# Pairs of heads normalised in one go, row maxima turned by VectorE, ten buffers of exponentials and an order written out as ranks, in a fused attention, soft-MoE and MLP kernel

## The chip, the core and the metric

One core of a Trainium2 chip runs one launch of the program. The metric is the device time of a run in microseconds; the profile gives the span from the first to the last instruction of one profiled execution. PE is TensorE's matmul side, PEld its weight loads, DVE VectorE, ACT ScalarE, POOL GpSimd, SP SyncE, whose queue issues most of the DMAs in its own order.

## The reference

```python
# q, k, v: [4, 8, 576, 64]
q_rot, k_rot = (rotate(q), rotate(k))                  # rotary embedding, halves of 32
scores = np.matmul(q_rot, k_rot.transpose(0, 1, 3, 2)) / np.sqrt(64)
attn = np.exp(scores - np.max(scores, axis=-1, keepdims=True))
attn = attn / (np.sum(attn, axis=-1, keepdims=True) + 1e-09)
x = np.matmul(attn, v)                                 # then [2304, 512], heads side by side
logits = x @ phi                                       # 32 slots: 8 experts x 4
d = softmax(logits, over tokens)                       # with 1e-09 in both sums
slot_out[e] = np.maximum((d.T @ x)[e] @ w1[e], 0.0) @ w2[e]   # e = 0..7, F = 1024
x = softmax(logits, over slots) @ slot_out
h = np.maximum(x @ w_in, 0.0)                          # w_in 512 x 2048, 64-bit words in memory
out = (h * h) @ w_out
```

## The kernel before

Attention works on sixteen pairs of heads (a batch has four). The two heads of a pair lie on partitions 0 to 63 and 64 to 127. The 576 keys are four blocks of 128 and a tail of 64, the 576 queries two halves of 288. One pair is nine units in the order of `SEQ`: blocks 0 to 3 for the first half, the tail for both halves (`BOTH`), blocks 0 to 3 for the second half. Rotary products are made on POOL (L424), rounded to a high part by ACT (L458), and the rest is kept as a low part.

For each unit three things run on PE. `max_unit` (L535) makes approximate scores from the high parts alone, and DVE reduces them to column maxima (L546). `st_unit` makes the scores from high and low parts (L607) and subtracts the row's maximum by one more matmul against `pick` (L614); ACT takes the exponential (L627) into one of the buffers `prs`. `pv_unit` multiplies an exponential with v (L655, the tail L650) into one of two PSUM banks, one for each half.

Between them stand smaller steps. `max_rows`, once a pair (twice in the first), reduces the maxima over the blocks (L558), turns the 128×10 result on PE (L565), copies it out on DVE with the second operand of the tail (L571, L576; `keep_apart` is a constant for that), and two DMAs put the row into `mrow` (L584), which the scores of this pair read. `norm`, once a half, lets PE sum the exponentials over the keys against ones (L676, eight calls), after POOL has added units 0 and 1 into an accumulator in `pb` (L635). DVE then transposes the sums in PSUM (L682), adds 1e-9 (L688), adds four quadrants crosswise (four L690), takes the reciprocal (L691), spreads it back by a transpose (L702) and multiplies (L698) into `xT`. `logits` then multiplies `xT` with phi (L726, L731) and turns it on PE (L749); `slots_in`, once a batch, forms the softmax over tokens and the slots' inputs (L794, L832). The experts (L1375, L1437) and the MLP (L1612, L1682) follow; their weights are loaded by SP into the buffers that attention gives up (L1002).

The order on every engine is made when the program is built. `Plan` holds all steps with the engine, the estimated length, what they read and write, and a due time, and emits at each moment the most urgent one that can start. `retime` sets the due times from tables (`TABLE`, `SHIFT`) and `STAY` lets PE prefer steps of the kind that it is in: r for approximate and exact scores, c and b for products with v, q for sums and logits, f for turning. Three pieces of PSUM, the ring, are taken by every step of PE that DVE or ACT reads afterwards, and given back by the reader. Buffers: six of exponentials for the blocks and two for the tail, and two accumulators in `pb`; `p_slot` numbers them round.

## Time and profile before

| | |
|---|---|
| runs, us | 569.60, 569.64, 570.91 (median 569.64) |
| span of the profiled execution, us | 567.9 |
| mean granted TensorE clock | 0.999 |
| busy, us: PE, PEld, DVE, ACT, POOL | 550.7, 419.7, 387.5, 285.4, 220.2 |
| DMA | 85.69 MB, mean 151 GB/s |

The profile is of one execution. The order in which to read it: the 40 slices and the windows by stage say which engine is full in which stretch; PE's timeline in one stretch gives the price of a step as the distance from one start to the next (ends of matmuls are modelled and overlap); the chain of waits says what the last instruction was waiting for, backwards; the groups give the mean time of one operation. Attention takes about the first 290 us, the experts the next 50, the MLP the rest.

### The profile page before, as it was taken

The numbers are of one execution on the slowest core, as the hardware profiler recorded it, in microseconds if no ns is written. First come the engines' busy times: TensorE is split into PE (matmuls) and PEld (weight loads), VectorE is DVE, ScalarE is ACT, GpSimd is POOL, SyncE is SP. The second block draws the span as 40 slices with busy tenths as digits, with TensorE's granted clock in tenths as the row PEclk, the third lists the DMA queues.
The fourth block names the chain that finished last, engine by engine and source line by source line (L and its number), as shares of the span: only waits on it lengthen the run. The fifth ranks groups of instructions, "written<-read, shape, count | busy, mean of one in ns | idle before, by whom it ended". The sixth has DMA issues, their size and how long they took to land.

```text
span 567.9 us, 13319 instructions
## 1 busy us (share of the span) xinstructions
PE 550.7 (97%) x5466; PEld 419.7 (74%) x5466; DVE 387.5 (68%) x845; ACT 285.4 (50%) x533; POOL 220.2 (39%) x173
## 2 busy tenths in 40 slices
PE   4999999999999999999999999999999999999996
PEld 3656666576666667666743348999999999999996
DVE  6587788888888877867475137975785595554553
ACT  2334455664565664534423247975944564454440
POOL 4999999987888888621200000000000000000000
PEclk9999999999999999999999999999999999999999
DMA  6547796867784356254669997142200220000333
GB/s 235 145 127 195 167 241 183 227 176 202 200 232 109 103 145 178 99 174 172 211 249 387 386 395 258 47 146 76 75 1 1 74 75 1 1 2 1 113 113 112
DMA packets 41838, 85.69 MB, mean 151 GB/s; under 512 B 12176, under 2 KB 12848, under 8 KB 40624
## 3 DMA queue, kind: packets, MB, share of 16 engines
q1 hardware_dynamic: 41494, 84.24, 47.9%
q8 instruction: 43, 0.70, 0.5%
q10 hardware_dynamic: 282, 0.59, 0.4%
q14 instruction: 19, 0.16, 0.1%
HBM read 77.92 MB, written 6.82 MB: 149 GB/s over the span
## 4 chain that ended last, share of the span: by engine, by line
PE 84%; DMA 5%; DVE 5%; POOL 2%; ACT 1%; issue 1%; SPq 0%; DVEq 0%
PE bank L1682 35%; PE bank L607 11%; PE obank L655 11%; PE bank L535 5%; PE bank L676 5%; PE bank L614 3%; PE obank L1612 3%; PE bank L1375 3%; DVE mcol L546 2%; DMA tEb<-in_w_dram 2%; DMA tLb<-in_w_in_dram 2%; PE obank L650 2%; PE bank L749 2%; DMA ident<-in_ident_dram 1%; POOL arena L424 1%; PE bank L726 1%
## 5 line engine op out<-in xcount | busy, mean ns | idle before, releaser
L627 ACT ACTIVATE tO<-bank 128x576 f32<-128x576 f32 x144 | 86.4, 650 | 87.0 <-PE bank L614 82.5
L546 DVE TENSOR_REDUCE mcol<-bank 128x2 f32<-128x576 f32 x144 | 103.2, 747 | 20.0 <-PE bank L535 10.0
L424 POOL TENSOR_TENSOR arena<-arena 128x576 f32<-128x576 f32 x78 | 110.9, 1441 | 8.1 <-DMA arena<-in_qk_dram 6.7
L1682 PE MATMUL bank<-w,tEb 128*128 128x256 f32 x864 | 106.6, 279 | 0.1
L1682 PEld LDWEIGHTS bank<-w,tEb 128*128 128x128 f32 x864 | 103.7, 188 | 2.3 <-issue 1.6
L655 PE MATMUL obank<-tO,pb 128*64 128x288 f32 x512 | 76.2, 419 | 0.0
L635 POOL TENSOR_TENSOR pb<-tO 128x576 f32<-128x576 f32 x32 | 45.7, 1429 | 36.2 <-ACT tO L627 34.4
L1682 PE MATMUL bank<-w,tEa 128*128 128x256 f32 x432 | 53.0, 278 | 0.0
L1682 PEld LDWEIGHTS bank<-w,tEa 128*128 128x128 f32 x432 | 51.6, 188 | 1.2 <-issue 1.2
L1682 PE MATMUL bank<-w,tO 128*128 128x256 f32 x432 | 51.6, 277 | 0.0
L1682 PEld LDWEIGHTS bank<-w,tO 128*128 128x128 f32 x432 | 51.1, 188 | 0.0
L655 PEld LDWEIGHTS obank<-tO,pb 128*64 128x64 f32 x512 | 31.1, 136 | 23.7 <-issue 9.5
L1623 ACT ACTIVATE pb<-obank 128x384 f32<-128x384 f32 x47 | 21.7, 494 | 38.0 <-PE obank L1612 37.9
L1623 ACT ACTIVATE w__1093<-obank 128x384 f32<-128x384 f32 x48 | 21.8, 492 | 36.9 <-PE obank L1612 36.6
L676 PE MATMUL bank<-tO,ones 128*32 128x288 f32 x256 | 36.7, 409 | 0.0
L535 PEld LDWEIGHTS bank<-tEb 64*128 64x128 f32 x180 | 16.3, 184 | 21.2 <-DVE mcol L546 4.2
L535 PE MATMUL bank<-tEb 64*128 64x288 f32 x180 | 30.8, 355 | 0.7 <-DVE mcol L546 0.5
L424 POOL TENSOR_TENSOR tLb<-arena,tEb 128x576 fp32r<-128x576 f32 x20 | 28.7, 1450 | 1.3 <-ACT tEb L458 1.3
L607 PE MATMUL bank<-tEb 64*128 64x288 f32 x180 | 28.3, 310 | 0.3 <-DVE mcol L546 0.2
L1612 PE MATMUL obank<-x,tO 128*128 128x384 f32 x95 | 26.8, 337 | 0.5 <-DVE tO L1540 0.5
L682 DVE STREAM_TRANSPOSE bank<-bank 128x288 f32<-128x288 f32 x32 | 15.9, 496 | 15.9 <-PE bank L676 15.8
L607 PE MATMUL bank<-tLb,tEb 64*128 64x288 f32 x180 | 26.6, 292 | 0.0
(309 smaller groups left out, 1066.8 us busy)
## 6 DMA issues: line engine op xcount, KB each, us to landing
arena<-in_qk_dram SPq DMA_DIRECT2D x14, 576.0 KB
arena<-in_qk_dram SPq DMA_DIRECT2D x12, 512.0 KB
arena<-in_w_dram SPq DMA_DIRECT2D x8, 512.0 KB
pb<-in_v_dram SPq DMA_DIRECT2D x12, 320.0 KB
arena<-in_qk_dram SPq DMA_DIRECT2D x3, 1152.0 KB
tLb<-in_w_in_dram SPq DMA_DIRECT2D x3, 1024.0 KB
pb<-in_w_in_dram SPq DMA_DIRECT2D x3, 1024.0 KB
w__450<-in_w_dram SPq DMA_DIRECT2D x4, 512.0 KB
```

The costliest lines, as they stand in the source:

```text
L424: ENG[e].tensor_tensor(out=o, in0=x, in1=y, op=how)
L535: nc.tensor.matmul(on_ring(tok)[:, j, 0:HQ], lhsT=x[rows], rhs=hi[rows, 0, HALF[c]], start=(u < BOTH or c == 0), stop=(u < BOTH or c == 1),)
L546: lambda e: nc.vector.tensor_reduce(out=mcol[:, h, :, u], in_=on_ring(tok)[:, :, 0:HQ], op=ALU.max, axis=AX.X),
L607: nc.tensor.matmul(st[:, j, 0:HQ], lhsT=w[rows], rhs=q[y][rows, HALF[c]], start=(i == 0 and (u < BOTH or c == 0)), stop=False,)
L614: nc.tensor.matmul(st[:, j, 0:HQ], lhsT=pick[rows, w : w + 128], rhs=mrow[rows, HALF[c]], start=False, stop=(u < BOTH or c == 1),)
L627: lambda e: nc.scalar.activation(out=pr, in_=on_ring(tok)[:, :, 0:HQ], func=AF.Exp, scale=0.125),
L635: lambda e: nc.gpsimd.tensor_tensor(out=acc, in0=one, in1=pr, op=ALU.add),
L655: nc.tensor.matmul(BANKS[6 + h][o, 0:HQ], lhsT=vr[:, u, j, :], rhs=pr[:, j, :], start=(h == 0 and u == 0), stop=(h == 1 and u == 3))
L676: nc.tensor.matmul(sm[QUAD[2 * j + w], 0:HQ], lhsT=one, rhs=xs_[2 * i + w][:, j, :], start=(i == 0), stop=(i == 1))
L1612: lambda e, i=i, t0=t0: nc.tensor.matmul(BANKS[i][:, 0:384], lhsT=wst_of()[:, 128 * fc : 128 * fc + 128], rhs=cst_of()[:, t0 : t0 + 384], ...
L1623: lambda e, i=i, h=h: nc.scalar.activation(out=rg_of()[:, 0, h], in_=BANKS[i][:, 0:384], func=AF.Relu),
L1682: nc.tensor.matmul(BANKS[c][:, cols], lhsT=gt[:, x, 128 * c : 128 * c + 128], rhs=wo[:, fc % 2, y, cols], start=(fc % FQ == 0 and i == 0 a ...
```

## The change

- **Order.** `retime` no longer moves due times by tables; it replaces each by a tenth of a rank out of `ORDER`, a list for each kind of step, engine and PE kind. `STAY` is gone.
- **Maxima.** `max_rows` stays on DVE: the tail's second operand is folded in by one more reduction, the result is turned by four 32×32 transposes, and the DMAs read that tile. The transpose on PE, the two copies, and `keep_apart` with its two instructions go.
- **Buffers.** `prs` has ten buffers: eight in the two `tO` tiles and two in `pb`, where the accumulators were. `slot_of` deals them out from a list; a buffer is given back early where POOL has added its contents into another. A score unit's matmuls now wait for the buffer's readers too.
- **Additions.** `fold` replaces the accumulators: POOL adds unit n into the buffer of unit 0, in place, for n below `folded(p)`: 2 for pairs 0 to 11, 4 for 12 to 14, 3 for the last. 46 additions stand for 32.
- **Norm.** Once a pair, after its last unit: one run of sums (16 matmul calls, 8 in pairs 12 to 14, 12 in the last), one transpose, the columns read out of PSUM by one instruction for both halves and four of 32 partitions, one reciprocal; then for each half the transpose back and the multiplication.

```diff
-    STAY = 20.522
+    ORDER = {
...
+        ("max_rows", "DVE", None): (
+            45, 55, 121, 216, 251, 336, 485, 597, 612, 688, 810, 895, 988, 1119, 1185, 1285, 1303
+        ),
...
-            kind, last = self.kinds[i] or (None, False)
-            key = (kind, "/".join(sorted(o[0])), {"b": "c"}.get(o[10], o[10]))
-            due = o[2]
-            if key in self.UNITS:
-                table, more, ahead = self.UNITS[key]
-                n = count[key] = count.get(key, -1 - ahead) + 1
-                if due >= -8 and (table != "mx" or n >= -3):
-                    due = n + self.TABLE[table + " last" if last and table != "mx" else table][n % 9] + more
-            elif due >= -8:
-                due += self.SHIFT.get((*key, last), self.SHIFT.get((*key, False), 0.0))
-            self.ops[i] = (*o[:2], due, *o[3:])
+            kind = self.kinds[i] and self.kinds[i][0]
+            key = (kind, "/".join(sorted(o[0])), kind and o[10])
+            n = count[key] = count.get(key, -1) + 1
+            ranks = self.ORDER.get(key, {})
+            if kind or n in ranks:
+                self.ops[i] = (*o[:2], 0.1 * ranks[n], *o[3:])
...
-                return o[2] - (self.STAY if c[3] == "PE" and o[10] is not None and o[10] == mode else 0.0), c[1], c[2]
+                return self.ops[c[2]][2], c[1], c[2]
...
-    NHI, NLO, NPR, NRING = 3, 3, 6, 10
+    NHI, NLO, NPR, NRING = 3, 3, 10, 10
...
-    accs = [view(pb, S * i, [128, 2, HQ]) for i in range(2)]
-    prs = [view(tos[i // 4], S * (i % 4), [128, 2, HQ]) for i in range(8)]
+    prs = [view(tos[i // 4], S * (i % 4), [128, 2, HQ]) for i in range(8)] + [view(pb, S * i, [128, 2, HQ]) for i in range(2)]
...
-            [ck], take="ring", tok=tok, mode="r",
+            [ck, (mk, u, h)], take="ring", tok=tok, mode="r",
...
     def max_rows(p, g, us=slice(0, 5)):
-        mr, mrk = small("mrow", [10, 128], F32R, bufs=2)
-        m10, m10k = small("m10", [128, 10])
+        mt, mtk = small("mrow", [32, 128], bufs=2)
         mcol, mk = mcols[p]
-        tok = {}
-        marks["r0"] = op(
-            {"DVE": 0.15},
-            lambda e: nc.vector.tensor_reduce(
-                out=m10.rearrange("p (j u) -> p j u", j=2)[:, :, us], in_=mcol.rearrange("p h j u -> p j u h")[:, :, us], op=ALU.max, axis=AX.X
-            ),
-            g + T["mrdve"], [(mk, u, h) for u in range(5)[us] for h in range(2 if u < BOTH else 1)], [m10k],
-        )
-        op(
-            {"PE": 0.11},
-            lambda e: nc.tensor.transpose(on_ring(tok)[0:10, 0, 0:128], m10, ident),
-            g, [m10k, "ident"], [("rw", p)], take="ring", tok=tok, mode="f",
-        )
-        op(
-            {"DVE": 0.25},
-            lambda e: nc.vector.tensor_scalar(out=mr, in0=on_ring(tok)[0:10, 0, 0:128], scalar1=1.0, scalar2=None, op0=ALU.mult),
-            g + T["mrdve"], [("rw", p)], [mrk],
-        )
-        marks["r1"] = ring_op(
-            {"DVE": 0.2},
-            lambda e: nc.vector.scalar_tensor_tensor(
-                out=mr[:, 0:64], in0=on_ring(tok)[0:10, 0, 64:128], scalar=keep_apart, in1=f(mr)[:, 0:64], op0=ALU.add, op1=ALU.max
-            ),
-            g + T["mrdve"], ["apart", ("rw", p)], [mrk], give="ring", tok=tok,
+        last = us.stop == 5
+        def turned(e):
+            if last:
+                nc.vector.tensor_reduce(out=mcol[0:64, 1, :, BOTH], in_=mcol[64:128, 0, :, BOTH].unsqueeze(2), op=ALU.max, axis=AX.X)
+            nc.vector.tensor_reduce(
+                out=m10[:, 0:10].rearrange("p (j u) -> p j u", j=2)[:, :, us], in_=mcol.rearrange("p h j u -> p j u h")[:, :, us], op=ALU.max, axis=AX.X
+            )
+            for a in range(4):
+                nc.vector.transpose(out=mt[:, 32 * a : 32 * a + 32], in_=f(m10)[32 * a : 32 * a + 32])
+        marks["r0"] = marks["r1"] = op(
+            {"DVE": 1.14 if last else 0.97}, turned,
+            g + T["mrdve"], [(mk, u, h) for u in range(5)[us] for h in range(2 if u < BOTH else 1)], ["m10", mtk],
         )
...
+    slot_of, idle, given = [], list(range(NPR)), []
+    def folded(p):
+        return 2 if p < NP - 4 else 4 if p < NP - 1 else 3
+    for n in range(NP * len(SEQ)):
+        p, i = divmod(n, len(SEQ))
+        idle += [x for t, x in given if t <= n]
+        given = [(t, x) for t, x in given if t > n]
+        slot_of.append(idle.pop(0))
+        u = SEQ[i][1]
+        given.append((n + 4 if 0 < u < folded(p) else 9 * p + 12, slot_of[-1]))
+        given.sort()
     def p_slot(p, h, u):
-        i = (8 * p + 4 * h + u) % NPR if u < BOTH else NPR + p % 2
+        i = slot_of[len(SEQ) * p + SEQ.index((h if u < BOTH else None, u))]
         return prs[i], ("P", i)
...
-            [ck], take="ring", tok=tok, mode="r",
+            [ck, pk], take="ring", tok=tok, mode="r",
...
-        if u == 1:
-            acc, ak = accs[(2 * p + h) % 2], ("acc", (2 * p + h) % 2)
-            one, k1 = p_slot(p, h, 0)
-            op(
-                {"POOL": 1.39},
-                lambda e: nc.gpsimd.tensor_tensor(out=acc, in0=one, in1=pr, op=ALU.add),
-                g + 0.6, [k1, pk], [ak],
-            )
...
+    def fold(p, h, n, s):
+        (pr, pk), (other, k) = p_slot(p, h, 0), p_slot(p, h, n)
+        op(
+            {"POOL": 1.39}, lambda e: nc.gpsimd.tensor_tensor(out=pr, in0=pr, in1=other, op=ALU.add),
+            s + n + 0.6, [k], [pk],
+        )
+    def norm(p, g):
+        things = [p_slot(p, None, BOTH)] + [[p_slot(p, h, u) for h in range(2)] for u in (0, *range(folded(p), 4))]
         tok = {}
         QUAD = [slice(32 * i, 32 * i + 32) for i in range(4)]
         def sums(e):
             sm = on_ring(tok)[:, 0]
-            xs_ = [acc] + [x for x, _ in rest]
-            for i in range(2):
+            for i, x in enumerate(things):
                 for j in range(2):
-                    for w in range(2):
-                        one = half_ones[:, h] if i and w else ones[:, 0:32]
+                    for h in range(2):
+                        one, pr = (ones[:, 0:32], x[h][0]) if i else (half_ones[:, h], x[0])
                         nc.tensor.matmul(
-                            sm[QUAD[2 * j + w], 0:HQ], lhsT=one, rhs=xs_[2 * i + w][:, j, :], start=(i == 0), stop=(i == 1)
+                            sm[QUAD[2 * j + h], 0:HQ], lhsT=one, rhs=pr[:, j, :], start=(i == 0), stop=(i == len(things) - 1)
                         )
-        op({"PE": 0.97}, sums, g + T["sums"], [("acc", n)] + [k for _, k in rest], [("sm", n)], take="ring", tok=tok, mode="q")
+        keys = [things[0][1]] + [k for x in things[1:] for _, k in x]
+        op({"PE": 0.485 * len(things)}, sums, g + T["sums"], keys, [("sm", p % 2)], take="ring", tok=tok, mode="q")
         op(
-            {"DVE": 0.47}, lambda e: nc.vector.transpose(out=on_ring(tok)[:, 1, 0:HQ], in_=on_ring(tok)[:, 0, 0:HQ]),
-            g, [], [("sm", n)],
-        )
-        def inverse(e):
-            col = on_ring(tok)[:, 1, 0:HQ].rearrange("p (b c) -> p b c", c=32)[:, :, 0:1]
-            nc.vector.tensor_scalar(out=r9, in0=col, scalar1=1e-9, scalar2=None, op0=ALU.add)
+            {"DVE": 0.5}, lambda e: nc.vector.transpose(out=on_ring(tok)[:, 1, 0:HQ], in_=on_ring(tok)[:, 0, 0:HQ]),
+            g, [], [("sm", p % 2)],
+        )
+        def columns(e):
+            col = on_ring(tok)[:, 1, 0:HQ].rearrange("p (b c) -> p c b", c=32)[:, 0:1]
+            nc.vector.tensor_scalar(out=r18, in0=col.to_broadcast([128, 2, HQ // 32]), scalar1=1e-9, scalar2=None, op0=ALU.add)
             for q in range(4):
-                nc.vector.tensor_tensor(out=r9[QUAD[q]], in0=r9[QUAD[q]], in1=col[QUAD[q ^ 1]], op=ALU.add)
-            nc.vector.reciprocal(out=r9, in_=r9)
-        def scaled(e):
+                nc.vector.tensor_scalar(out=r18[QUAD[q], 1 - q % 2], in0=col[QUAD[q ^ 1], 0], scalar1=1e-9, scalar2=None, op0=ALU.add)
+        def scaled(e, h):
             parts = [(slice(0, 128), 0, HQ, HQ * h)]
             if p < TURNED:
                 parts = [(HEADS[0], 0, HQ, HQ * h)] + [(HEADS[1], a, b, (HQ * h + a - 64) % S) for a, b in (((0, 64), (64, HQ)) if h == 0 else ((0, HQ),))]
             for rows, a, b, to in parts:
                 nc.vector.tensor_tensor(out=xT[rows, to : to + b - a], in0=BANKS[6 + h][rows, a:b], in1=recT[rows, a:b], op=ALU.mult)
-        ring_op({"DVE": 1.1}, inverse, g, [("sm", n)], ["r9"], give="ring", tok=tok)
-        op(
-            {"DVE": 0.48}, lambda e: nc.vector.transpose(out=recT, in_=r9.to_broadcast([128, HQ // 32, 32])),
-            g, ["r9"], ["recT"],
-        )
-        op(
-            {"DVE": 0.8 if p < TURNED else 0.4},
-            scaled,
-            g, [("O", h), "recT"], [("xT", h)],
-        )
+        ring_op({"DVE": 0.8}, columns, g, [("sm", p % 2)], ["r18"], give="ring", tok=tok)
+        op({"DVE": 0.27}, lambda e: nc.vector.reciprocal(out=recs, in_=r18), g, ["r18"], ["r9"])
+        for h in range(2):
+            op(
+                {"DVE": 0.48}, lambda e, h=h: nc.vector.transpose(out=recT, in_=recs[:, h].unsqueeze(2).to_broadcast([128, HQ // 32, 32])),
+                g + 0.1 * h, ["r9"], ["recT"],
+            )
+            op(
+                {"DVE": 0.8 if p < TURNED else 0.4},
+                lambda e, h=h: scaled(e, h),
+                g + 0.1 * h, [("O", h), "recT"], [("xT", h)],
+            )
...
-            if n in ENDS:
-                at(s + LAG + 0.1, norm, p, ENDS[n], s + T["norm"])
+            if u == 0:
+                for i in range(1, folded(p)):
+                    at(s + LAG + 0.5, fold, p, h, i, s)
+        at(g0 + NU - 1 + LAG + 0.1, norm, p, g0 + NU - 1 + T["norm"])
...
```

How the order moves, at three places. In its rows `tEa`, `tEb` and `tLa`, `tLb` are the high and the low parts of the rope results, `es` stands in the matmuls that only fill PE's time, `obank` is a bank of products with v, `tO` and `pb` hold exponentials, `w__` a load buffer. A count behind a row stands for like rows.

PE at the start, before, from the first pair's tail maxima on:

```order
L535 MATMUL bank_93<-tEa,wins 128x288 x2
L565 MATMUL bank_91<-ident,m_115 10x128
L1756 MATMUL obank_94<-es 128x128 x4
L565 MATMUL bank_91<-ident,m_115 10x128
L607 MATMUL bank_92<-tEa 128x288 x2
L607 MATMUL bank_92<-tLa,tEa 128x288 x2
L607 MATMUL bank_92<-tEa,tLa 128x288 x2
L614 MATMUL bank_92<-tEb,pick 128x288 x2
L607 MATMUL bank_93<-tEa 128x288 x2
L607 MATMUL bank_93<-tLa,tEa 128x288 x2
L607 MATMUL bank_93<-tEa,tLa 128x288 x2
L614 MATMUL bank_93<-tEb,pick 128x288 x2
```

and after the change:

```order
L644 MATMUL bank_93<-tEa,wins 128x288 x2
L1863 MATMUL obank_94<-es 128x128 x6
L719 MATMUL bank_91<-tEa 128x288 x2
L719 MATMUL bank_91<-tLa,tEa 128x288 x2
L719 MATMUL bank_91<-tEa,tLa 128x288 x2
L726 MATMUL bank_91<-tEb,pick 128x288 x2
L719 MATMUL bank_93<-tEa 128x288 x2
L719 MATMUL bank_93<-tLa,tEa 128x288 x2
L719 MATMUL bank_93<-tEa,tLa 128x288 x2
L726 MATMUL bank_93<-tEb,pick 128x288 x2
L644 MATMUL bank_92<-tEb 128x288 x2
L644 MATMUL bank_91<-tEb 128x288 x2
```

The two transposes of the maxima (L565) are gone from PE, and behind the second score unit (`bank_93`) stand maxima of the next pair (L644 on `tEb`), where before the third of five score units followed.

POOL at the start, before, from the second low part of pair 1 (`tLb`) on; L635 is the addition of exponentials:

```order
L424 TENSOR_TENSOR tLb<-arena,tEb 128x576
L424 TENSOR_TENSOR arena<-arena,w__134 128x576
L635 TENSOR_TENSOR pb<-tO_83 128x576
L424 TENSOR_TENSOR arena<-arena 128x576
L424 TENSOR_TENSOR arena<-arena,w__134 128x576
L424 TENSOR_TENSOR tLb<-arena,tEb 128x576
L424 TENSOR_TENSOR arena<-arena,w__134 128x576
L635 TENSOR_TENSOR pb<-tO_84 128x576
L424 TENSOR_TENSOR arena<-arena 128x576
L424 TENSOR_TENSOR arena<-arena,w__134 128x576
L424 TENSOR_TENSOR tLb<-arena,tEb 128x576
```

and after, with L768 for the additions:

```order
L534 TENSOR_TENSOR tLb<-arena,tEb 128x576
L534 TENSOR_TENSOR arena<-arena,w__132 128x576 x3
L534 TENSOR_TENSOR arena<-arena 128x576 x2
L768 TENSOR_TENSOR tO_83<-tO_83 128x576
L534 TENSOR_TENSOR tLb<-arena,tEb 128x576
L534 TENSOR_TENSOR arena<-arena,w__132 128x576
L768 TENSOR_TENSOR tO_84<-tO_84 128x576
L534 TENSOR_TENSOR tLb<-arena,tEb 128x576
L534 TENSOR_TENSOR arena<-arena,w__132 128x576 x3
```

The rope of pair 2 (the rows on `arena` up to its second one without `w__`) stood behind one addition and around a low part, and now stands ahead of both.

PE behind the last score unit, before, from the turning of pair 14's result on:

```order
L749 MATMUL bank_93<-ident,pb 128x128 x4
L749 MATMUL bank_93<-ident,pb 64x128
L655 MATMUL obank_94<-tO_83,pb 64x288 x4
L650 MATMUL obank_94<-tO_84,pb 64x288 x2
L650 MATMUL obank_95<-tO_84,pb 64x288 x2
L655 MATMUL obank_95<-tO_84,pb 64x288 x4
L655 MATMUL obank_95<-tO_83,pb 64x288 x4
L726 MATMUL bank_91<-pb,phi_sb 32x128 x4
L731 MATMUL bank_91<-pb,phi_sb 32x64 x4
L749 MATMUL bank_93<-ident,pb 128x128 x4
L749 MATMUL bank_93<-ident,pb 64x128
```

and after, from pair 14's logits to the last pair's:

```order
L837 MATMUL bank_92<-pb,phi_sb 32x128 x4
L842 MATMUL bank_92<-pb,phi_sb 32x64 x4
L785 MATMUL bank_93<-tO_84,half_ones 32x288 x4
L785 MATMUL bank_93<-pb,ones 32x288
L785 MATMUL bank_93<-tO_84,ones 32x288
L785 MATMUL bank_93<-pb,ones 32x288
L785 MATMUL bank_93<-tO_84,ones 32x288
L785 MATMUL bank_93<-tO_83,ones 32x288
L785 MATMUL bank_93<-tO_84,ones 32x288
L785 MATMUL bank_93<-tO_83,ones 32x288
L785 MATMUL bank_93<-tO_84,ones 32x288
L837 MATMUL bank_91<-pb,phi_sb 32x128 x4
```

The last pair's sums (L785, before L676) stood ahead of its last products with v (L655); now they stand behind all of them, between the logits of pair 14 and those of the last pair. In SP's row the last four loads of experts' weights into `arena` have moved behind the four into `tEb` and `tLb`, just ahead of those into `tEa`.

## Rows read from the trace of the kernel before

**Rows 1.** Windows: stretch, length, busy us (records) of PE PEld DVE ACT POOL, PEclk, DMA, GB/s.

```profile
20.00:40.00 20.00, 19.64 (x190) 12.90 (x190) 11.52 (x31) 9.84 (x19) 18.70 (x15) 1.00 0.45 122
180.00:200.00 20.00, 20.00 (x240) 13.03 (x234) 17.65 (x45) 9.68 (x19) 16.60 (x13) 1.00 0.57 138
```

**Rows 2.** PE's timeline, 195.8 to 212: start us, us, engine, line, operation, shapes.

```profile
197.18 0.29 PE L535 MATMUL bank<-tEb 64*128 64x288 f32 x2
197.41 1.68 PE L655 MATMUL obank<-tO,pb 128*64 128x288 f32 x12
199.01 0.40 PE L535 MATMUL bank<-tEb 64*128 64x288 f32 x2
199.25 0.29 PE L535 MATMUL bank<-tEb,wins 64*128 64x288 f32 x2
199.38 0.29 PE L607 MATMUL bank<-tEb 64*128 64x288 f32 x2
...
202.92 0.28 PE L565 MATMUL bank<-ident,m 128*10 128x128 f32 x1
203.03 0.76 PE L749 MATMUL bank<-ident,pb 128*128 128x128 f32 x5
...
209.73 0.71 PE L655 MATMUL obank<-tO,pb 128*64 128x288 f32 x4
210.37 0.40 PE L535 MATMUL bank<-tEa 64*128 64x288 f32 x2
```

**Rows 3.** Chain of waits that ended last: start us, us, what, instructions.

```profile
234.64 0.65 PE obank L650 x8
...
270.29 1.94 PE bank L676 x32
...
317.47 10.75 DMA tEb<-in_w_dram
```

**Rows 4.** Windows at the end of attention, columns as in rows 1.

```profile
284.00:288.00 4.00, 4.00 (x40) 2.05 (x35) 3.46 (x14) 0.75 (x2) 0.00 (x0) 1.00 0.12 44
292.00:296.00 4.00, 3.56 (x30) 2.02 (x30) 3.71 (x18) 1.46 (x7) 0.00 (x0) 1.00 1.05 392
```

**Rows 5.** Groups by form on DVE: xcount, then busy us, mean ns, then idle before.

```profile
L690 DVE TENSOR_TENSOR r<-r,bank 32x9 f32<-32x9 f32 x128 | 20.7, 162 | 2.4
...
L682 DVE STREAM_TRANSPOSE bank<-bank 128x288 f32<-128x288 f32 x32 | 15.9, 496 | 15.9 <-PE bank L676 15.8
```

**Rows 6.** Timeline of all engines, 16 to 27; SPq is a DMA issued by SP.

```profile
16.39 0.17 DVE L558 TENSOR_REDUCE m<-mcol 128x6 f32<-128x12 f32 x1
...
18.35 3.30 SPq L584 DMA_DIRECT2D tEb<-mrow  x2
...
20.29 0.61 PE L607 MATMUL bank<-tEa 64*128 64x288 f32 x2
...
22.14 1.41 POOL L424 TENSOR_TENSOR arena<-arena 128x576 f32<-128x576 f32 x1
22.37 0.44 PE L607 MATMUL bank<-tEa 64*128 64x288 f32 x2
...
25.99 0.44 PE L535 MATMUL bank<-tEb 64*128 64x288 f32 x4
```

**Rows 7.** Timelines of PE, SP and DVE at the last score and after it.

```profile
279.79 0.29 PE L614 MATMUL bank<-tEa,pick 64*128 64x288 f32 x2
...
288.74 0.41 PE L726 MATMUL bank<-pb,phi_sb 128*32 128x128 f32 x4
...
288.86 0.46 DVE L698 TENSOR_TENSOR pb<-obank,pb 128x288 f32<-128x288 f32 x1 [1.10 <-PE obank L655]
...
287.93 1.92 SPq L1002 DMA_DIRECT2D tO<-in_w_dram  x4
```

**Rows 8.** Groups on POOL, the addition of exponentials.

```profile
L635 POOL TENSOR_TENSOR pb<-tO 128x576 f32<-128x576 f32 x32 | 45.7, 1429 | 36.2 <-ACT tO L627 34.4 <-DMA arena<-in_qk_dram 1.6
```

**Rows 9.** The page's 40 slices, POOL's busy tenths.

```profile
POOL 4999999987888888621200000000000000000000
```

## What the change does to the time: the prediction

> **What bounds the kernel now.** I read the windows by stage first, then TensorE's (PE's) own timeline inside the busiest one, then the groups by form for the operations that the change touches, and last the two ends of the attention part. The windows say that PE is the bound of attention: in the stretch 180 to 200 us it is busy 20.00 of 20.00 us with 240 matmul records, while VectorE (DVE) has 17.65, GpSimd (POOL) 16.60 and ScalarE 9.68 [rows 1]. The PE timeline in the same place shows start following start with no idle note [rows 2], so each PE instruction removed there is worth its own time and no more. The stretch 20 to 40 us is the other kind: 190 records, and POOL has 18.70 of 20.00 [rows 1]; there the rope of the next pair, on POOL, sets the pace. After attention the chain of waits goes through a DMA, 10.75 us at 317.47 [rows 3], and the loads move 392 GB/s with a DMA share of 1.05 in 292 to 296, against 44 GB/s in 284 to 288 [rows 4]: the stage of the experts waits for weights. So there are three parts: middle (PE), start (POOL and the first waits), end (DMA). The span of the profiled execution is 567.9 us and the median of the runs 569.64, so 1.74 us lie around the span; I make the sum against the span and add 1.74.
>
> **Prices on PE, from the timeline.** Two matmul calls of the scores' kind cost .13 (199.25 to 199.38). Leaving that kind for another costs .23 − .13 = .10 (197.18 to 197.41), and the first call pair after the return .24 − .13 = .11 (199.01 to 199.25), .21 for an excursion. Three units of the product with v take 1.60 (197.41 to 199.01), one takes .64 (209.73 to 210.37): .48 for a unit, .24 a call, and .16 that each run of another kind costs however long it is; I take .15. One transpose of the maxima costs .11 (202.92 to 203.03) [rows 2]. Sixteen calls of the sums cost 1.94, .121 a call [rows 3].
>
> **What PE loses.** (a) The maxima of each pair are turned by DVE: 17 transposes on PE go, 17 × .11 = 1.87. (b) The sums of a pair run once. For twelve pairs they are still 16 calls; for pairs 12 to 14, with more exponentials added up beforehand, 8; for the last, 12: 256 calls become 228, 28 × .121 = 3.39. (c) With fewer steps of another kind, PE's row has 128 runs outside the scores' kind instead of 138 and leaves that kind 72 times instead of 76 (counted in the order): 10 × .15 + 4 × .21 = 2.34. Together 7.6 us. About 1.0 of it (four calls of the sums, two calls of the products) lies behind the last score, where PE does not set the end; 6.6 lie in the saturated part. **Term: −6.6.**
>
> **What the other engines get.** Of DVE's norm one transpose of 496 ns goes in each pair, and of eight additions of 162 ns four stay, reading PSUM directly [rows 5]: .50 + 4 × .16 = 1.1 us less, at least, since one of two reciprocals goes too. The maxima gain four small transposes for two copies, about +.4. Both lie beside PE's 16.2 us per pair (sixteen pairs between 20.29 and 279.79 [rows 6, 7]), of which DVE already leaves over 10% free. At nothing, then, as long as DVE does not answer late. A rule speaks against (a), though: the Trainium skill, "VectorE: DVE Perf Modes", "Rules for kernel authors", sends a 128×128 transpose to TensorE where PSUM will do as its destination, and keeps VectorE for 32×32 blocks; four blocks stand for one instruction here. By it DVE would get more small instructions for no gain; by the rows PE is full and DVE is not, and the sum stays.
>
> POOL adds in place. Per pair up to 11 it has the same two additions as before, each 1429 ns [rows 8]; the last four have fourteen more, 14 × 1.43 = 20 us, in slices where the page shows POOL falling from 8 tenths to 6, 2, 1, 2 [rows 9]. That cover is enough for all but the last pair's.
>
> **The start.** The first maxima are reduced at 16.39 + .17, and the DMA that carries the turned row starts at 18.35, 1.8 us later, with PE and its fill matmuls between; the first score is at 20.29 [rows 6]. Four small DVE transposes take that place. No row shows a 32×32 one; the nearest ones are 162 ns for a tiny DVE operation and 496 for a 128×288 transpose [rows 5], so .65 to 2.0, and I take .8, nearer to the small one since a block has a thirty-sixth of the elements: the first score about 1 us earlier. But the new order puts only two score units ahead of the next pair's maxima, where the old one has five. These maxima wait for rope that POOL ends at 22.14 + 1.41 and ScalarE has still to round, and ran at 25.99 [rows 6]; PE would be through with two units by about 21.3 and stand for 2 to 4 us. In return POOL gets pair 2's last rope result sixteenth instead of nineteenth in its row, 3 × 1.43 = 4.3 us earlier, in just the stretch where it sets the pace, and the claimed maxima start earlier. The stretch 20 to 40 lacks 50 records of the 240 a full one has, 50 × 20/240 = 4.2 us [rows 1]: more than that cannot be won. **Term: −1, ends −4.2 and +4.** The upper end is the clock: the matmul at 22.37 is busy .44 where that of the same kind at 199.38 is .29 [rows 2, 6], so PE starts slow though the granted clock of the stretch reads 1.00 [rows 1], and a pause there may keep it slow for longer. The Trainium skill, "TensorE: Matmul & The Clock Gate", "Part 1: The HAM clock gate", has a cold array at 1.2 GHz and a busy one at 2.4; by it the early stop would cost doubled matmuls for some microseconds, which is this upper end; half of the chance of no change below is for it.
>
> **New waits in the middle.** The order is fixed: where one engine is late, nothing moves up. In the new code a score unit's matmuls wait for the buffer's readers, not only its exponential, the sums need one slot in PSUM for the whole pair, and DVE's five norm steps stand between maxima. No stall in [rows 2] shows such a wait; below it is bounded by 0 (ten buffers instead of six and two), above by about one more excursion, .21 and what stands idle at it, for each of sixteen pairs, 4 us; I take the lower half, since PE's row has fewer runs than before and so more work of one kind at hand. **Term: +1.5.**
>
> **The end.** The last score ends at 279.79 + .13 (call it t0); the last logits begin at 288.74, t0 + 8.8, and the second half is normalised by 288.86 + .46 [rows 7]. Now all products come first: behind t0 stand 16 calls × .24 [rows 2], .65 of the split unit [rows 3], .76 of transposes (203.03), some .4 of a pair's logits (288.74) and 12 × .121 of sums, with about .5 of changes 7.6 us; POOL's four additions, 4 × 1.43 from about t0 + .8, are done at 6.5 and fit. Then DVE: a transpose of .50, six small steps × .162, again .50 [rows 5] and .46, with handing over 2.8, and .96 for the second half: normalised at t0 + 11.4 where it was t0 + 9.4, 2 us later on PE. But the loads into the buffers of the exponentials, which start the saturated DMA stretch, went out at 287.93, t0 + 8.0 [rows 7], and those buffers are free at t0 + 7.6 now, so DMA starts no later, and it sets the end of that stage [rows 3, 4]. The 2 MB of experts' weights that were loaded into the arena long before are issued some 8 us before t0 by the new order; 2 MB at 392 GB/s are 5.4 us and fit into a time in which DMA is nearly idle (44 GB/s [rows 4]). **Term: +.5, ends −.5 and +5.4.**
>
> **Sum.** −6.6 − 1 + 1.5 + .5 = −5.6; 567.9 − 5.6 = 562.3, and with 1.74 **564.0 us**.
>
> **Rivals.** *Better* (.20): the start wins its full 4.2 and no new wait comes: −6.6 − 4.2 + .5 = −10.3, 559.4. For it speaks that POOL's pace is the start's limit; against, that PE is left without work at 21. *No change* (.17): the clock or the stop at the start costs +4, or the arena's loads come too late by 5.4; −6.6 + 4 + 1.5 + .5 gives 569.0, with the loads −6.6 − 1 + 1.5 + 5.4 gives 568.9. For: PE's slow matmuls in [rows 6]; against: the idle DMA before 288. *Slower* (.13): an addition in place may not write before PE's product with v has read the old values, so POOL, which runs in order, stands in front of the rope behind it. POOL has 3.40 of 20 us free [rows 1], 2.75 for each 16.2; two waits a pair are covered up to 1.4 us each. From there on they count. If each waits for one unit, 16.2 / 9 = 1.8, a pair loses .85, eleven pairs 9.4: 562.3 + 9.4 + 1.74 = 573.4. Against it: in the order the first addition of a pair stands well behind the product that it waits for; the second stands right behind its own. That the change does not do what it says can be ruled out from the order: 17 transposes and 28 calls are gone from PE's row.
>
> **Chances.** Forecast (562 to 567) .50, better .20, no change .17, slower .13. A measurement here tells about .3%, 1.7 us, from no change: 567.9 to 571.4 is no change. Faster .70, same .17, slower .13. The range leaves out the slower case and the edges of the others, 2 in 10 in all: from just under the better case, 559.0, to just over no change, 569.5.
>
> **What would show it.** Right: no PE transposes of the maxima; 228 calls of the sums; a pair period of about 15.8 instead of 16.2; the last score 6 to 8 us before 279.79; first score near 19.3. The start term is wrong if the 20 to 40 stretch has fewer than 190 records, or if busy .44 matmuls go on beyond 24 us. The middle term is wrong if PE shows idle released by DVE or ScalarE in 180 to 200. The end term is wrong if the distance from the last score to the DMA-bound chain of the experts grows by over 1 us. The slower rival shows as POOL idle released by PE in front of additions.

## The result and the profile after

The changed kernel takes 578.17 us (median of 4 runs, 576.23 to 580.03) against 570.0: a ratio of 1.0128, 95% interval [1.0081, 1.0174], slower where I forecast faster. Its profiled execution spans 574.4 us (before 567.9). Where the 6.5 us between the two spans came from:

| us | before | after | difference |
|---|---|---|---|
| start to first score matmul | 20.29 | 23.11 | +2.8 |
| first to last score | 259.50 | 258.65 | −.85 |
| last score to the experts' first matmul | 16.5 | 20.5 | +4.0 |
| experts, to the MLP's first matmul | 44.0 | 43.9 | −.1 |
| MLP to the end | 227.6 | 228.3 | +.7 |

I had written −1 for the first line, −5.1 for the second and +.5 for the third. Each column is one execution. Four executions that share the order after (this one, e0, e3 and e14 below) have 256.8 to 258.7 us from first to last score and the last score at 280.1 to 281.8, never ahead of 279.79. The windows of after that answer to [rows 1], and two behind the last score:

```profile
20.00:40.00 20.00, 19.51 (x186) 14.00 (x186) 15.26 (x33) 8.09 (x15) 20.00 (x15) 0.89 0.47 144
180.00:200.00 20.00, 19.76 (x245) 11.92 (x249) 16.27 (x42) 10.59 (x24) 17.55 (x13) 1.00 0.50 116
290.00:300.00 10.00, 6.26 (x42) 3.06 (x44) 6.26 (x23) 2.43 (x10) 0.00 (x0) 0.71 0.89 324
300.00:310.00 10.00, 10.00 (x84) 4.42 (x76) 6.94 (x31) 2.07 (x5) 0.53 (x1) 0.95 0.85 293
```

The last two stretches before:

```profile
290.00:300.00 10.00, 9.01 (x72) 4.32 (x75) 6.68 (x29) 3.43 (x12) 0.53 (x1) 1.00 1.05 393
300.00:310.00 10.00, 10.00 (x79) 3.59 (x71) 6.14 (x28) 2.88 (x7) 0.00 (x0) 1.00 1.05 387
```

In 290 to 300 TensorE (PE) has 42 matmul records instead of 72, the granted clock is .71 instead of 1.00 (a mean between the two levels of 1.2 and 2.4 GHz), and DMA, saturated before, has .89 and then .85.

**The start.** What SP issues first in after, and the rope on DVE that waits for it:

```profile
0.74 0.61 SPq L587 DMA_DIRECT2D pb<-in_v_dram  x1
1.41 0.61 SPq L519 DMA_DIRECT2D arena<-in_qk_dram  x1
2.06 1.55 SPq L587 DMA_DIRECT2D pb<-in_v_dram  x2
3.65 0.62 SPq L519 DMA_DIRECT2D arena<-in_qk_dram  x1
```

```profile
7.74 1.43 DVE L534 TENSOR_TENSOR arena<-arena,w__132 128x576 f32<-128x576 f32 x2 [4.89 <-DMA arena<-in_qk_dram]
```

Three loads of v stand ahead of or between the loads of q and k, and rope starts at 7.74 (before 6.36). That is half of it. Ahead of the first maxima PE runs 16 matmuls that nobody reads (`warm_up`); they wait for a product of the rope that DVE makes second in its row before and fifth after. First before, then after:

```profile
7.84 3.78 PE L1766 MATMUL obank<-arena 128*128 128x128 f32 x16 [7.84 <-DVE arena L424]
```

```profile
11.36 3.46 PE L1873 MATMUL obank<-arena 128*128 128x128 f32 x16 [11.36 <-DVE arena L534]
```

They start 3.6 us behind the rope's start where it was 1.5. ScalarE, too, can round the second high part only at 13.21, before at 10.77.

**The middle.** PE's recorded waits from 23 to 282 us, by place (engine, line, waited for: us, times, longest); first after, then before:

```profile
PE bank L644 <- DVE mcol L655: 1.5, 2, 0.9
PE bank L719 <- DVE mcol L655: 0.8, 3, 0.4
PE bank L719 <- ACT tO L739: 0.7, 2, 0.4
PE bank L943 <- DVE mcol L655: 0.4, 1, 0.4
```

```profile
PE bank L535 <- DVE mcol L546: 0.5, 2, 0.3
PE bank L607 <- DVE mcol L546: 0.2, 1, 0.2
PE bank L535 <- ACT tO L627: 0.2, 1, 0.2
```

All rows together: 4.9 us after, .9 before. The view shows only part. I summed the time from each PE matmul's start to the next one's, by kind, over all records between first and last score (us; two experiments from below beside it). "Whole" are the products of the blocks of 128 keys, "split" those of the tail:

| kind | before | after | e11 | e17 |
|---|---|---|---|---|
| maxima and scores | 128.0 | 128.5 | 126.7 | 129.9 |
| products with v, whole | 67.0 | 70.9 | 66.9 | 67.1 |
| products with v, split | 9.7 | 9.7 | 18.4 | 11.0 |
| sums | 32.8 | 28.3 | 32.8 | 32.8 |
| logits | 5.0 | 6.6 | 5.0 | 5.1 |
| transposes of outputs | 10.7 | 10.7 | 12.8 | 10.8 |
| transposes of maxima | 2.3 | 0 | 0 | 0 |
| slots | 4.0 | 4.0 | 4.0 | 4.0 |
| sum | 259.5 | 258.7 | 266.6 | 260.8 |

What was taken away did go: 4.5 of sums, 2.3 of transposes. But 3.9 came back on the products, 1.6 on the logits, .5 on the scores.

**The end.** PE behind the last score in after, the experts' first matmul, and the loads of the next experts' weights on SP:

```profile
292.87 0.41 PE L837 MATMUL bank<-pb,phi_sb 128*32 128x128 f32 x4 [3.04 <-DVE pb L807]
...
297.90 2.52 PE L943 MATMUL bank<-x,es 128*32 128x512 f32 x16
...
302.24 0.62 PE L1482 MATMUL bank<-w__490,sit 128*32 128x512 f32 x2
```

```profile
291.94 4.54 SPq L1113 DMA_DIRECT2D pb<-in_w_dram  x4
303.33 0.37 SPq L1113 DMA_DIRECT2D w__490<-in_w_dram  x1
```

In the kernel before:

```profile
297.36 0.37 SPq L1002 DMA_DIRECT2D w__450<-in_w_dram  x1
```

PE stands 3.04 us for VectorE's (DVE's) chain; then the clock is down (.50 from 295 to 301) and 16 matmuls take 2.52. A buffer of the experts' weights can be loaded again only when PE has used it, so these loads move with PE: 303.33 instead of 297.36, six microseconds, of which the later last score is two. DMA runs dry meanwhile: its share is 0.00 from 303 to 304.

### The profile page after: what moved, and what is told of

Same layout as the page of the kernel before. It is cut to its first block, busy times and chain, and to the rows that moved or that the text cites. A ratio compares the mean times of both kernels' runs of the same rounds, so it can differ in the third digit from the quotient of the medians.

```text
span 574.4 us, 13090 instructions
## 1 busy us (share of the span) xinstructions
PE 546.2 (95%) x5397; PEld 418.4 (73%) x5397; DVE 382.6 (67%) x783; ACT 283.1 (49%) x531; POOL 240.4 (42%) x187
## 4 chain that ended last, share of the span: by engine, by line
PE 76%; DMA 7%; DVE 6%; POOL 6%; ACT 3%; issue 1%; SPq 1%; DVEq 0%; ACTq 0%
PE bank L1789 33%; PE bank L719 9%; PE obank L759 9%; POOL arena L534 4%; PE bank L785 4%; PE bank L644 4%; DMA w__1019<-in_w_in_dram 3%; PE obank L1719 3%; PE bank L726 3%; PE bank L1482 3%; DVE mcol L655 2%; DMA tLb<-in_w_in_dram 2%; PE bank L860 2%; PE bank L1544 1%; PE bank L943 1%
## 5 line engine op out<-in xcount | busy, mean ns | idle before, releaser
L655 DVE TENSOR_REDUCE mcol<-bank 128x2 f32<-128x576 f32 x144 | 102.4, 751 | 32.3 <-PE bank L644 25.4
L534 POOL TENSOR_TENSOR arena<-arena 128x576 f32<-128x576 f32 x78 | 111.7, 1456 | 10.7 <-DMA arena<-in_qk_dram 9.7
L739 ACT ACTIVATE tO<-bank 128x576 f32<-128x576 f32 x128 | 77.5, 652 | 74.6 <-PE bank L726 60.0
L759 PE MATMUL obank<-tO,pb 128*64 128x288 f32 x448 | 66.8, 418 | 0.4 <-ACT tO L739 0.4
L759 PEld LDWEIGHTS obank<-tO,pb 128*64 128x64 f32 x448 | 27.6, 136 | 24.6 <-issue 9.4
L768 POOL TENSOR_TENSOR pb<-pb,tO 128x576 f32<-128x576 f32 x22 | 31.0, 1410 | 18.5 <-PE obank L759 7.9
L768 POOL TENSOR_TENSOR tO<-tO,tO 128x576 f32<-128x576 f32 x21 | 30.5, 1451 | 1.1 <-PE obank L759 0.7
L719 PE MATMUL bank<-tEb 64*128 64x288 f32 x180 | 29.5, 324 | 1.4 <-ACT tO L739 0.7
L534 POOL TENSOR_TENSOR tLb<-arena,tEb 128x576 fp32r<-128x576 f32 x20 | 28.2, 1423 | 0.1
L644 PE MATMUL bank<-tEb 64*128 64x288 f32 x180 | 26.4, 336 | 1.5 <-DVE mcol L655 0.9
L719 PE MATMUL bank<-tEb,tLb 64*128 64x288 f32 x180 | 26.5, 291 | 0.0
L644 PEld LDWEIGHTS bank<-tEb 64*128 64x128 f32 x180 | 15.3, 184 | 15.1 <-DVE mcol L655 5.7
```

The lines of the kernel that those rows point to most:

```text
L534: ENG[e].tensor_tensor(out=o, in0=x, in1=y, op=how)
L644: nc.tensor.matmul(on_ring(tok)[:, j, 0:HQ], lhsT=x[rows], rhs=hi[rows, 0, HALF[c]], start=(u < BOTH or c == 0), stop=(u < BOTH or c == 1),)
L655: lambda e: nc.vector.tensor_reduce(out=mcol[:, h, :, u], in_=on_ring(tok)[:, :, 0:HQ], op=ALU.max, axis=AX.X),
L719: nc.tensor.matmul(st[:, j, 0:HQ], lhsT=w[rows], rhs=q[y][rows, HALF[c]], start=(i == 0 and (u < BOTH or c == 0)), stop=False,)
L739: lambda e: nc.scalar.activation(out=pr, in_=on_ring(tok)[:, :, 0:HQ], func=AF.Exp, scale=0.125),
L759: nc.tensor.matmul(BANKS[6 + h][o, 0:HQ], lhsT=vr[:, u, j, :], rhs=pr[:, j, :], start=(h == 0 and u == 0), stop=(h == 1 and u == 3))
```

## The experiments

Most of them first work out a kernel's order, a list `seq` of steps with their engines, and then replay it with some steps moved; the diffs show the move in short. Every time is a median beside runs of the kernel before in the same session (570.0 to 571.0).

**e0, e1: the start.** e0 replays the changed kernel's order with nothing moved; e1 issues the first q and k loads ahead of v.

```diff
- v, qk, v, v, qk, ...
+ qk, qk, ..., v, v, v, ...   (SP's first ten loads)
```

> The changed kernel again, with its sequence worked out first and then written down, nothing moved: every theory expects the changed kernel's time, 576 to 580 us against 570 before, and a profile like it: first score at 23.1, last score 281.8, first matmul of the experts 302.2. It is the base for the other runs.

> On SP the first loads of q and k stand ahead of the first loads of v, as they did before; nothing else moves. Theory S1 (the late start is carried to the end): rope on VectorE starts 1.4 us earlier, the first score at about 20.3 instead of 23.1, and the time falls by 2 to 3 us. Theory S2 (the stretch up to 70 us is paced by POOL and has room, so that the late start is caught up in any case): the first score at 20.3, but the time falls by under 1 us.

578.29 (1.0120 [1.0076, 1.0164]) and 578.99 (1.0120 [1.0078, 1.0161]). But e1 undoes only a part of the late start: rope begins at 6.55, PE's 16 matmuls still wait until 10.16, and the first score comes at 21.92 (e0 22.56, after 23.11), not at 20.3 as both theories had it. So neither is tested as meant. The .6 us ahead of e0 are gone by 147 us and not seen in the time; executions of one order differ from each other by more than that on the way. GpSimd (POOL), 20.00 of 20.00 us busy in the first window above (before 18.70), could be what takes them up; no run shows it. What the rest of the late start costs at the end stays open.

**e2, e3: the end.** e2 puts the last pair's sums, without POOL's additions, ahead of its last products; e3 only fills PE's pause with 12 matmuls that nobody reads.

```diff
-        return 2 if p < NP - 4 else 4 if p < NP - 1 else 3
+        return 2 if p < NP - 4 else 4 if p < NP - 1 else 1
+    # in seq: the last pair's sums and DVE's steps ahead of its last five products
```

```diff
+    seq[at + 1 : end] = [(None, "PE", None)] * 12 + between   # fill, behind the last sums
```

> The last pair's sums run on PE ahead of most of its products with v, as they did before, and take 20 matmul calls instead of 12, since nothing is added up on POOL for this pair. Theory T1 (the late end of the last norm holds up the experts' first matmuls, and with them the loads into the buffers that these read): no 3 us hole on PE ahead of the last logits, the experts' first matmul at 297 to 299 instead of 302.2, the time lower by 3 to 4 us. Theory T2 (the DMA rate sets the end of that stage): PE's hole goes, but the time falls by under 0.7 us.

> The changed kernel with 12 fill matmuls on PE between the last pair's sums and its logits, where PE stands for 3 us; nothing else moves. Theory C1 (in that hole the granted clock falls, and the slots' inputs and the turning behind it run at half rate, L943 at 2.5 us for 16 records instead of 1.35): the clock of the stretch 290 to 300 reads 1.00, the experts' first matmul comes 1.2 to 2 us earlier and the time falls by as much. Theory C2 (the clock's part is hidden): the clock reads 1.00 and the time falls by under 0.5 us.

574.07 (1.0038 [1.001, 1.0065]) and 573.64 (1.0058 [1.0026, 1.009]). Windows of e2, then of e3:

```profile
290.00:300.00 10.00, 8.92 (x84) 4.88 (x84) 6.66 (x27) 2.76 (x11) 0.53 (x1) 1.00 0.78 267
```

```profile
290.00:300.00 10.00, 7.99 (x75) 4.96 (x77) 6.85 (x25) 2.76 (x11) 0.53 (x1) 1.00 1.03 382
```

Either mends over half of the loss. e3 changes no step that the result needs, only whether PE is at work; the clock stays at 1.00, and the gain is 4.7 us where I had expected 1.2 to 2. The end's price was more the clock behind the pause than the longer chain: the 16 matmuls of L943 take 1.42 in e3, and what is left there, 19.0 us from the last score to the experts' first matmul instead of 16.5, is the chain. The mean clock of whole executions says the same: .981 to .987 in e0, .990 to 1.00 in e2, mostly .993 to .994 in e3.

**e7: a shorter chain.** DVE's four additions of the other tensor's sums are left out, so the denominators lack that tensor.

```diff
-            for q in range(4):
-                nc.vector.tensor_scalar(out=r18[QUAD[q], 1 - q % 2], in0=col[QUAD[q ^ 1], 0], ...)
```

> The changed kernel without the four additions of the other tensor's sums on VectorE (32 partitions each), so the denominators are incomplete; the order of all that is left is the same. VectorE has .75 us less per pair, 12 us in all, and PE the same work. Theory D1 (PE waits between 80 and 180 because VectorE's chain of norm and maxima answers late): 3 to 6 us less than the changed kernel. Theory D2 (the waits follow from the fixed order and from loads, not from the length of VectorE's chain): under 1 us less, most of it from the last pair's chain.

576.58 (1.0096 [1.0071, 1.0122]): 1.7 us of the 8 in all sixteen pairs, between the two theories. The length of DVE's norm is at most a small part of it.

**e4, e9: the experts' weights.** The changed order loads 5 MB of them between 82 and 165 us, among the pieces of the MLP's weights, for which ScalarE waits there. e4 moves each behind the store of the piece ahead of it, e9 moves them behind 199 and 218 us.

```diff
+    seq: each load of experts' weights behind the store of the w_in piece ahead of it   # e4
+    seq: two of them behind the seventh store, three behind the last                    # e9
```

> Between 80 and 165 us the 1 MB loads of experts' weights that stand right behind a piece of w_in on SP are moved behind that piece's store, so they no longer share the DMA engines with it. Theory M1 (these loads hold up the pieces of w_in, ACT and VectorE wait for them in order, and the maxima and exponentials behind them come late): ACT's waits on that DMA fall from 4.7 us to under 1 us and the time falls by 1.5 to 3 us. Theory M2 (PE's waits between 90 and 190 come from VectorE's own work in the new order, not from the DMA): ACT's waits go, the time falls by under 0.7 us.

> The changed kernel with 5 MB of experts' weights moved on SP from the stretch 80 to 165 us to two places behind 195, where the DMA share is .3 to .5; nothing else moves. Theory M1 (between 80 and 180 the pieces of w_in and the loads of q and k share the DMA engines with these loads, and ACT, VectorE and POOL wait for them in order): ACT's and POOL's waits on loads fall by 5 us or more, the last score comes 2 to 4 us earlier, and the time falls by 2 to 4 us. Theory M2 (the middle is lost by PE and VectorE waiting for each other in the fixed order): under 0.7 us.

582.52 (1.019 [1.0149, 1.023]) and 583.24 (1.0222 [1.019, 1.0254]), both worse. The waits (e4's POOL from 23 to 282, e9's PE from 200 to 282):

```profile
POOL arena L568 <- DMA arena<-in_qk_dram: 13.8, 5, 4.9
```

```profile
PE bank L760 <- DMA tEb<-mrow: 3.1, 1, 3.1
```

Moved loads run into the q and k loads, or into the small DMA that carries the maxima. Neither run takes the waits away as theory M1 wanted: ScalarE's waits for the pieces, 5.1 us after the change, are 9.4 in e4 and 3.5 in e9. In e9 PE's work was .6 us ahead of e0's by 220 us, no more. That speaks against the loads as what held the middle and doesn't settle it.

One more run, e10, had the last pair's sums ahead as in e2, q and k first as in e1 and the weights late as in e9. Expected were 569 to 571 if the loads held the middle and 573 to 575 if not; it took 577.75 (1.0125 [1.0092, 1.0158]), neither. Its last score comes at 286.5 as in e9 (286.0), with a wait of 3.0 us for the same small DMA: the late loads cost what the end gained.

**e5, e6: the order written out.** e5 gives the changed steps to the planner of before; e6 gives it the maxima step alone.

```diff
-    ORDER = {...}    # the rank table
+    UNITS = {...}    # the table, shifts and stay of before (e5)
```

> All steps of the changed kernel, but ordered by the due times, tables and the preference for one kind that the kernel before has; only the table of ranks is undone. Theory O1 (the steps are worth what the prices said, and the written order loses it between 80 and 180 us and at the start): first score at about 19.5 to 20.5, the stretch 80 to 180 at least as fast as before, the last score at 276 to 279, and unless the end is late here too a time of 564 to 571. Theory O2 (the steps themselves make PE wait, in any order): the last score at 281 or later and a time of 575 or more.

> The kernel before with one part of the change: the maxima's rows are turned by VectorE, with no transpose on PE and no copies; rules, norm and buffers stay as they were. Theory P1 (PE is full and VectorE is not, so a transpose off PE is worth its .11 and its place in the order): 1.5 to 3 us less than before. Theory P2 (VectorE answers later by as much as PE is spared): within 0.7 us of before. Theory P3 (the order that the old rules make of it is worse): slower by over 1 us.

598.86 (1.051 [1.0465, 1.0555]) and 611.17 (1.0709 [1.0678, 1.074]): POOL waits 28.2 and 28.6 us for q and k (before 6.7). By their numbers e5 is theory O2 and e6 is P3. But e6 and e8, the next run, hold the same step and differ by 25.6 us: that much is the replanned order and not the step, and e5 can't tell the two apart either. The next runs hold the order.

**e8, e11, e14: maxima on DVE, and the places of the tiles.** e8 replays before's own sequence with the turning done by DVE and nothing in PE's place. e11 is e8 with every tile at its address in the kernel before: e8's new tile had pushed all later ones, the weight tiles among them, 64 bytes on. e14 does that to the changed kernel.

```diff
-            lambda e: nc.tensor.transpose(on_ring(tok)[0:10, 0, 0:128], m10, ident),
+            # e8, e11: in the reduction's step on DVE, behind it
+            for a in range(4):
+                nc.vector.transpose(out=mt[:, 32 * a : 32 * a + 32], in_=f(m10)[32 * a : 32 * a + 32])
```

```diff
+    pool.tile([128, 16], F32, name="spare64")      # e14, else the changed kernel
     m10 = pool.tile([128, 32], F32R, name="m10")
```

> The kernel before with its own sequence on every engine, out of which only the 17 transposes of the maxima on PE, the copies behind them and the two instructions of the constant are taken, with VectorE's reduction and four small transposes in the place of the first reduction. No rule plans anew. Theory P1 (PE is full, so each transpose off PE is worth its .11 and its share of a change of kind): 1.5 to 3 us less than before. Theory P2 (VectorE answers later by what PE is spared): within 0.7 us of before. That it is slower by more than 1 us neither expects; then the 40 us that the planned version lost would be the step's and not the plan's.

> The run with only the maxima step, in the order of the kernel before (585.6 us), with every tile at the address that it has in the kernel before; there the small tile of the maxima had pushed all later tiles, the experts' and the MLP's weights among them, 64 bytes further. Theory P (places): the 8.7 us that the MLP stage had lost (236.3 against 227.6 us) were the places; the stage comes back to 228 us, its matmuls of 256 columns from 283 to 278 ns, and the time to about 577. Theory S (step): something the step left behind (a queue, the clock) slows the MLP; the stage stays at 236 and the time at 585. Both expect the 5 us lost in the attention to stay, since that is VectorE's chain of 1.2 us in one piece where one instruction of 0.15 stood.

> The changed kernel in its own order, with 64 unused bytes per partition ahead of the small tiles, so that these and all weight tiles of experts and MLP lie 64 bytes further. Theory P: the MLP stage goes from 228.3 to about 237 us, its matmuls of 256 columns from 278 to 283 ns, the time to about 587, and the attention stays as it is. Theory S: no change, 578.

585.55 (1.0267 [1.0235, 1.0299]), which neither theory had, 576.92 (1.0108 [1.0082, 1.0134]) and 586.38 (1.0266 [1.0236, 1.0296]). The places were worth 8.6 us in one kernel and 8.2 in the other, all of it in the MLP, whose instructions nobody touched. 450 to 500 us of before, then of e14 (columns as in [rows 1]):

```profile
450.00:500.00 50.00, 50.00 (x431) 48.80 (x430) 33.28 (x49) 26.87 (x45) 0.00 (x0) 1.00 0.08 28
```

```profile
450.00:500.00 50.00, 50.00 (x411) 49.39 (x411) 30.60 (x42) 25.46 (x42) 0.00 (x0) 1.00 0.13 43
```

At the same granted clock PE gets through 411 matmuls where it had 431. What is left in e11 is the step itself, +6 us; the table above has it at the split products, 18.4 instead of 9.7. That line of e11, and DVE there:

```profile
L684 PE MATMUL obank<-tO,pb x128: 402/428/454, 28.6 to 292.3; 64*64 64x288 f32 x128
its engine sat idle before it (us, times) until:
  DVE pb L732: 7.3, 14
```

```profile
168.52 0.47 DVE L736 STREAM_TRANSPOSE pb<-r 128x288 f32<-128x288 f32 x1
169.02 0.15 DVE L587 TENSOR_REDUCE mcol<-mcol 64x2 f32<-64x2 f32 x1
169.21 0.17 DVE L588 TENSOR_REDUCE m<-mcol 128x10 fp32r<-128x20 f32 x1
169.42 0.84 DVE L592 STREAM_TRANSPOSE mrow<-m 32x32 f32<-32x32 f32 x4
170.29 0.46 DVE L732 TENSOR_TENSOR pb<-obank,pb 128x288 f32<-128x288 f32 x1
```

The normalisation (170.29) empties the PSUM bank into which PE's split product goes next, and four transposes of .84 in all stand in front of it, once in each pair.

**e17: the four transposes behind the normalisation**, where the two copies out of PSUM had stood.

```diff
+        def blocks(e):          # now the step of the first copy; the reduction stays where it was
+            for a in range(4):
+                nc.vector.transpose(out=mt[:, 32 * a : 32 * a + 32], in_=f(m10)[32 * a : 32 * a + 32])
```

> The kernel before in its own order and places, with the maxima turned by VectorE, the four transposes of each pair not in front of the normalisation of the pair's second half but behind it, where the two copies out of PSUM stood (e11, with them in front, gave 576.9 us). Theory L (VectorE's late answer at this one place is the whole loss): the split products go from 18.4 us between first and last score back to 9.7, the transposes of the outputs from 12.8 to 10.7, the stretch from 266.6 to about 256; with 1 us of it lost where VectorE still has 0.3 to 0.4 us a pair more, the time is about 567, under the kernel before (570.6). Rival N (VectorE answers late at other places then): 572 or more.

570.5 against 570.7 (.9999 [.9975, 1.0023]): 6.4 us back by one place on DVE, and the wait at that line is gone:

```profile
L686 PE MATMUL obank<-tO,pb x128: 402/428/453, 28.4 to 286.5; 64*64 64x288 f32 x128
its engine sat idle before it (us, times) until:
  issue: 1.9, 10
```

But not under the kernel before, as theory L wanted; 570.5 lies between the two theories. In the profiled execution (574.1, e17's slowest) the last score comes at 279.98, before at 279.79; what that execution took above the median lies behind it. Up to it, 1.3 stay at the split products and 1.9 more at the scores, and eat the 2.3 us of transposes that PE lost.

PE's weight loads show where the first of these comes from. The place is that of [rows 2], where I had read the price of a transpose of the maxima: the transposes of the outputs (L749, L785) with the transpose of the maxima (L565) ahead of them in before and nothing ahead of them in e17, and ScalarE's exponentials (L627, L663) beside them. Before:

```profile
201.78 1.19 ACT L627 ACTIVATE tO<-bank 128x576 f32<-128x576 f32 x2
202.91 0.09 PEld L565 LDWEIGHTS bank<-ident,m 128*10 128x10 f32 x1 [0.44 <-ACT tO L627]
203.02 0.42 PEld L749 LDWEIGHTS bank<-ident,pb 128*128 128x128 f32 x4
```

and in e17:

```profile
201.84 1.19 ACT L663 ACTIVATE tO<-bank 128x576 f32<-128x576 f32 x2
203.08 0.42 PEld L785 LDWEIGHTS bank<-ident,pb 128*128 128x128 f32 x4 [0.54 <-ACT tO L663]
```

The exponentials end at 202.97 and at 203.03, and the transposes of the outputs start .05 behind them both times. They take a piece of the ring that the exponential gives back. In before this distance is .05 at all eleven places where a transpose of the maxima stands ahead of them, in e17 at ten of the eleven. So the transpose of the maxima filled a wait that was there anyway, and without it 1.0 of the 1.3 us that these eleven had taken comes back as that wait. The rest goes elsewhere: e17's first score comes at 19.15, 1.1 us ahead of before, and that lead is gone by 205 us, in waits for ScalarE near 65 and 90 us and for DVE's maxima near 199.

**e12, e13: PE's waits in the changed order.** They come back at the same places in six runs of this order, 4.7 us on average. e12 turns round five of them, 2.5 us; e13 adds e2's end.

```diff
+    pairs = [([pv[8]], st[13]), ([norm[5]], mx[77]), ([pv[62]], mx[89]), ([pv[71]], st[83]), ([norm[8]], slots[0])]
+    # in seq: the left step directly ahead of the right one
```

> The changed kernel with five places turned round on TensorE, at which it waited in every run of its order for VectorE or ScalarE (0.33, 0.83, 0.56, 0.40 and 0.40 us, 2.5 together): the unit that waited goes behind the next one of other work. Theory M (the middle lost by waits that can be covered): the last score comes about 2 us earlier after the first, time near 576. Rival C (VectorE is as late as TensorE all along, and a wait taken out returns at the next place): the recorded waits stay near 5 us and the time is within 0.7 us of the changed kernel's 578.2.

> The five turned places together with the last pair's sums ahead of its last products (which alone gave 574.1 us). If the two parts of the loss are separate: theory M 572, rival C 574. In both the clock stays at 1.00 from 290 on and the experts' first matmul comes about 15 us after the last score.

579.69 (1.0145 [1.0116, 1.0174]) and 573.66 (1.0045 [1.0026, 1.0064]). Waits of e12's PE, 23 to 282:

```profile
PE bank L768 <- DVE m L849: 1.6, 2, 1.4
PE bank L768 <- DVE mcol L704: 1.3, 3, 0.9
PE bank L834 <- DVE mcol L704: 1.0, 1, 1.0
...
PE obank L808 <- ACT pb L788: 0.7, 1, 0.7
```

5.8 us in all: by the waits rival C, though e12 is 1.5 us above 578.2 where C had it within .7. The sums put in front (L834) wait for the same DVE reduction, the product (L808) for an exponential. In e13 e2's gain stays and nothing is added.

**e15, e16: which places.** e13 with the weight tiles 32 bytes further, and with all tiles from the tables on 32 bytes back.

```diff
+    pool.tile([128, 8], F32, name="spare")     # e15
-    recs = pool.tile([128, 32], F32, name="recs")...
+    recs = pool.tile([128, 24], F32, name="recs")...     # e16
```

> The kernel with five turned places and the last pair's sums ahead of its last products (573.7 us), with 32 unused bytes ahead of the small tiles: the weight tiles of experts and MLP lie 32 bytes further, the activations where they were. Theory D (the distance between the weights and the activations decides: 64 bytes further cost 8.2 us, 32 is half of the way): the MLP stage goes from 229 to between 229 and 237 us, time 574 to 582. Theory A (the address decides, and one that is a multiple of 64 is better): the stage falls below 229 us and the time below 573; how far no run shows.

> The same kernel with the table of reciprocals 32 bytes shorter: all tiles behind it, activations and weights, lie 32 bytes nearer to the start, at multiples of 64, with the distances that they had. Theory D: no change, MLP stage 229 us, time 573.7 within 1 us. Theory A: the stage falls below 229 us, further than where only the weights moved, and the score stage may move too.

580.11 (1.0131 [1.0089, 1.0173]) and 574.0 (1.0031 [1.0003, 1.0059]): 6.4 us lost where the distance between weights and activations changed, nothing where all moved together. That is theory D of the two. That the weights' own address decides by another rule, good at its place and 32 bytes below it and worse 32 and 64 above, fits the four placements as well and was not tested apart. None of the placements tried was better than the one that both kernels have. No version came out clear of the kernel before on the faster side.

## Why the prediction was wrong, point by point

- **The bound.** That PE is saturated and "each PE instruction removed there is worth its own time and no more" is the step that failed. Of the 6.8 us that went, 6.0 came back between first and last score. For the 2.3 of the transposes e17 shows how: with DVE's work at the best place found it is as slow as before. 1.0 came back on the spot, where the next step waited for ScalarE's exponential in any case; the .11 that I read at 202.92 [rows 2] was such a wait, not a price. The rest, with a first score 1.1 us earlier, went into waits for ScalarE and DVE further on. For the 4.5 of the sums the table shows where the time came back, on products and logits, but no run shows that it had to. A busy row doesn't show how close the next answer is.
- **What PE loses.** Sums and transposes came off in full: 6.8 by the table, where I had 5.3 for them and 2.34 for fewer runs of another kind, 1.0 of all that behind the last score. But a run that goes passes its price on to its neighbour: the logits had been followed by sums and changed over to them at little cost; now they pay for their own exit, +1.6.
- **What the others get.** "At nothing, then, as long as DVE does not answer late" names the condition and then passes over it. I priced the four small transposes at .8 and they take .84; where they stand on DVE was worth 6.4 us (e11, e17). The rule that I weighed, in the Trainium skill, "VectorE: DVE Perf Modes", "Rules for kernel authors", to use TensorE for a 128×128 transpose where PSUM will do as destination, would have come nearer: e17 shows no gain from leaving it.
- **The start.** −1, measured +2.8. I read the orders of PE and POOL and neither SP's first rows, in which v is loaded ahead of q and k, nor DVE's first rope products, for one of which those 16 matmuls wait. The four small transposes did what I had said: in e17, without the new order, the first score comes 1.1 us earlier. The clock fell as the upper end had it (.89 in 20 to 40, [rows 1] 1.00). How much of the +2.8 reaches the end no run shows; e1 takes back .6 to 1.2 of it and gains nothing.
- **New waits.** +1.5, bounded by 4. The table shows 6.0 coming back, 1.6 of it behind the logits (mostly their exits, with a wait of .4), about .5 one more product unit inside the stretch, the rest waits; the view of waits has 4.0 more than before. Turning five of them round gained nothing (e12). Whether another order of the same steps would save them stays open.
- **The end.** The times themselves were near: sums over at t0 + 7.9 (7.6), normalised at t0 + 11.8 (11.4). The step that failed is "DMA starts no later, and it sets the end of that stage": only the first loads start no later, the next ones wait for PE. And a pause of 3 us on PE took the clock with it, a price that I had for the start and not for here.
- **Rivals.** "Slower" was to come from POOL standing in front of additions; POOL waits 7.9 us in two places for PE, the longer one, 5.6 us, behind its last rope, and its rope is ahead of before's from 26 to about 100 us. The result lies outside of the range, above, by causes that none of the cases held together: the end, of which e2 and e3 each take back about 4.5, and a start and a middle that together never brought the last score forward.

## What to carry to other kernels

An engine that is busy all the time in a fixed order is not yet the bound: ask for each instruction that goes what the one behind it was waiting for, and for each that moves to another engine what stands right behind it there, and who waits for that. Where a chain at a stage's end leaves TensorE without work for some microseconds, count the clock behind it too, and follow the loads that wait for TensorE. When an added or removed tile shifts others in SBUF, compare the untouched stages first.

## What the runs showed of the hardware that was not expected

- Where the weights lie in SBUF against the activations changes the rate of matmuls: the mean of the 256-column matmuls on `tEb` in 400 to 500 us, in the MLP, is 278 ns in before and after, 281 with the weights 32 bytes further (e15), 283 with 64 (e14), 279 with all moved 32 bytes the other way (e16). In before and in e14:

```profile
L1682 PE MATMUL bank<-w,tEb 128*128 128x256 f32 x417 | 50.7, 278 | 0.0
```

```profile
L1816 PE MATMUL bank<-w,tEb 128*128 128x256 f32 x360 | 45.2, 283 | 0.0
```

  Three to five nanoseconds on each of some 1,890 records are 6 to 9 us over the stage; 6.4 to 8.6 were measured. Whether it is the distance or the weights' own address, and what conflict lies behind it, no run shows.
- The clock behind PE's pause of 3.04 us: .71 over 290 to 300, and .56 and .76 over 290 to 300 and 300 to 310 in e0. Twelve matmuls in the pause kept it at 1.00. A pause is not the only occasion: e17's profiled execution has .66 there with no pause of that size.

```profile
290.00:300.00 10.00, 9.22 (x56) 4.88 (x56) 6.96 (x29) 2.83 (x11) 0.53 (x1) 0.66 1.04 391
```

- A 32×32 transpose on DVE takes 199 ns (median of 68 after the change), where one of 128×288, thirty-six such blocks, takes 496 [rows 5]. So the time grows far less than the number of blocks.
